# A small VectorE instruction with a destination in three rows instead of one run

## The chip, the core and the metric

The kernel runs on one core of a Trainium2 chip. A core has five engines that work side by side, each through its own list of instructions in a fixed order: TensorE (PE in the profile; its weight loads are PEld), VectorE (DVE), ScalarE (ACT), GpSimd (POOL) and SyncE (SP, which here issues most of the DMAs). They wait for one another through semaphores. The metric is the time of one execution on the device, in microseconds. Before the change it is 1541.81 us, the median of three runs (1540.87 to 1546.98).

## The reference

Two steps, one behind the other: attention that keeps the 32 largest scores of each row, and a mixture of eight experts on its output.

```python
def _attn_ref(q, k, v):                      # q, k, v: (8, 8, 576, 64)
    scores = scale * np.matmul(q, k.transpose(0, 1, 3, 2))
    kth = np.partition(scores, -32, axis=-1)[..., -32:-31]
    mask = scores >= kth
    scores = np.where(mask, scores, -1e9)
    ...                                      # softmax over the kept scores
    return np.matmul(attn, v)

def _moe_ref(x, w_gate, w1, w2):             # x: (4608, 512), 8 experts
    logits = x @ w_gate
    order = np.argsort(-logits.flatten())    # greedy: best pairs first, at most 576 tokens an expert
    ...
    out[mask] = np.maximum(x[mask] @ w1[e], 0.0) @ w2[e]   # for each expert
```

## The kernel before

**Stages.** The attention takes the first 1076 us or so, then come the routing and the experts. The change touches the attention alone.

**Tiles.** The 64 heads are taken in 32 pairs. The two heads of a pair have 2 x 576 rows of scores, that is nine tiles of 128 rows and 576 columns; tile 4 holds the last 64 rows of both heads. Each tile goes through the same steps (function `tile_ops`). The names in brackets are those that rows of the trace show, with their lines:

- TensorE writes the scores to PSUM (`s`, L449), in f16 pairs of high and low parts. Four such score areas are in use at a time.
- VectorE takes the eight largest of each of six chunks of 96 columns (`cd`, L453 and L454), and out of these 48 candidates the eight largest three times, blanking what it has found in between (MAX8 at L457, L459, L461, MATCH_REPLACE8 at L458, L460). So it has the 24 largest in `st`.
- ScalarE marks with a sign which scores lie above the 24th (`w`, L466) and adds the signs up in a column of `acc`: with them it is known how many scores reach the threshold.
- VectorE makes the **fill** (`fw`, L476): it compares a small table `tab` of constants with that column. The result are eight numbers, each 0 or a tiny negative one.
- TensorE pushes the marked scores far down (`s<-w,off`, L471), and adds the fill, multiplied by the same large constant (`s<-fw,off`, L472), to eight spare columns beside the scores.
- VectorE takes the eight largest of the 584 columns that are now there (MAX8, L473). They end with the 32nd largest score.
- ScalarE makes a mask of what lies under it (`r`, L479). TensorE turns scores and masks round and adds them up (`pt`, L515 to L521), ScalarE takes the exponential (`F`, L525), and GpSimd splits it into high and low f16 parts (`ehm`, L528, and `elm`, L531). TensorE multiplies these with the values (`pv`, L622).

**A loop over three tiles.** The largest score of a row, known after L457, goes into the queries that the turned products use. For every three tiles of a pair GpSimd copies the maxima into the queries (`nq`, L500), and a DMA on SyncE's queue transposes them (`Qt<-nq`, L501). Products of later tiles read them (`s<-kz,Qt`, L449). So a pair has three such transposes, 96 in all.

**What sets the order.** A planner (class `Loom`) sorts the operations of each engine by a table of numbers (`TAU`), one list for each engine, and the program is issued in that order. Within an engine the order is fixed; only semaphores decide when an instruction starts. The planner adds spare matmuls where TensorE would stand idle for long (function `stay`).

**Buffers.** The fill's tile has four buffers, the table is made once, at the kernel's start, by an iota on GpSimd.

Of the kernel before, what the change touches and what calls it, by code (L numbers as in the profile page):

```python
# [9 lines left out]
F32 = mybir.dt.float32  # L10
F32R = mybir.dt.float32r
F16 = mybir.dt.float16
BF16 = mybir.dt.bfloat16
# [3 lines left out]
ALU = mybir.AluOpType  # L17
# [193 lines left out]
def attention(tc, q,k,v,w_gate,x_out,L,acc,cuts, pairs,ahead=()):  # L211
# [3 lines left out]
    with ExitStack() as ctx:  # L215
        ctx.enter_context(tc.manual_schedule())
        cp=ctx.enter_context(tc.tile_pool(name="cp",bufs=1))
        io=ctx.enter_context(tc.tile_pool(name="io",bufs=2))
        wk=ctx.enter_context(tc.tile_pool(name="wk",bufs=2))
# [3 lines left out]
        V,G,A,T=nc.vector,nc.gpsimd,nc.scalar,nc.tensor  # L223
        SS=[ps_s.tile([128,1536],F32,name=f"s{j}") for j in range(LANES//2)]
        def part(slot,kind,x,e):

            j,a=slot%(LANES//2),slot//(LANES//2)
            tc.add_to_no_dep_group(f"{j}{a}{kind}{e}",x.ins)
            for g in {"o":(f"{j}{1-a}o",f"{j}{1-a}m",f"{j}{1-a}t",f"{j}{a}t"),"t":(f"{j}{1-a}o",f"{j}{a}o"),"m":(f"{j}{1-a}o",)}[kind]:
                for o in "VAP":  # L230
                    if o!=e: tc.declare_no_dep(x.ins,group=g+o,reason="another bank")
            return x
        identf=cp.tile([128,128],F32,name="identf"); make_identity(nc,identf)
        off=cp.tile([128,128],BF16,name="off"); V.tensor_scalar_mul(off,identf,-(2.0**79))
        out_=cp.tile([128,128],BF16,name="out_"); V.tensor_scalar_mul(out_,identf,-(2.0**48))
        keep=cp.tile([128,128],BF16,name="keep"); V.tensor_scalar_mul(keep,identf,2.0**127)

        tab=cp.tile([128,8],F32,name="tab")
        G.iota(tab,[[2,8]],base=2*24-576,channel_multiplier=0,allow_small_or_imprecise_dtypes=True)
        wg=cp.tile([128,4,8],F32,name="wg")  # L240
        wgr=cp.tile([128,2,2,8],F32,name="wgr")
        wv=w_gate.rearrange("(g r a d) e -> a r d g e",g=2,r=2,a=2,d=64)
# [5 lines left out]
        for i in range(2):  # L248
            t=cp.tile([128,2,9,128],F16,name=f"nq{i}"); NQ.append(t); V.memset(t[:,1,:,64:128],0.0)
            t=cp.tile([128,2,9,128],F16,name=f"nk{i}"); NK.append(t); V.memset(t[:,1,:,65:128],0.0); V.memset(t[:,1,:,64:65],-QS)  # L250
# [178 lines left out]
        def tile_ops(P,i):  # L429
# [3 lines left out]
            col=slice(n*9+i,n*9+i+1)  # L433
            D={}
            def at_(): return D["at"]["slot"]
            def side(): return at_()//(LANES//2)
            def span(a,b):

                s_ps=SS[at_()%(LANES//2)]; o=960*side()
                return s_ps[:,o+a:o+b]  # L440
# [4 lines left out]
            def products(Q,K,n_,o,k0,kind,first,last):  # L445
                for h in ([0] if i<4 else ([1] if i>4 else [0,1])):
                    if i==4: rows=slice(h*64,h*64+64); qc=slice(512+h*64,576+h*64)
                    else: rows=slice(0,128); qc=slice(i*128,i*128+128)
                    part(at_(),kind,T.matmul(o[rows],P[Q][:n_,qc],P[K][:n_,k0(h):k0(h)+o.shape[1]],start=first,stop=last,skip_group_check=True),"P")  # L449
# [17 lines left out]
            def move(half):  # L467
                u=side(); o=64*u if half else 512*(1-u); n_=512 if half else 64
                if not half:
                    for Q,K,k0 in (("Q1","K2",512),("Q2","KZ",0)): products(Q,K,128,span(o,o+64),lambda h: k0+64*h,"t",Q=="Q1",False)  # L470
                part(at_(),"o" if half else "t",T.matmul(span(o,o+n_),off,P["w"][i][:,o:o+n_],start=False,stop=bool(half),skip_group_check=True),"P")  # L471
                if not half: part(at_(),"t",T.matmul(span(-8,0) if u else span(576,584),off,D["fw"],start=False,stop=True,skip_group_check=True),"P")  # L472
            def next8(): part(at_(),"m",V.max(P["st"][:,i,24:32],span(-8,576) if side() else span(0,584)),"V")  # L473
            def fill():
                D["fw"]=wk.tile([128,8],BF16,tag="fw",name="fw",bufs=4)
                V.tensor_scalar(D["fw"],tab,acc[:,col],-2.0**-39,op0=ALU.is_lt,op1=ALU.mult)  # L476
            def relu():
                r=wk.tile([128,576],BF16,tag="r",name="r",bufs=WPB); P["r"][i]=r
                part(at_(),"m",A.activation(r,span(0,576),AF.Relu,bias=P["st"][:,i,31:32],scale=-1.0),"A")  # L479
# [8 lines left out]
            p=go("nt",minus,[p],e="A",d=.092,late=.1)  # L488
            p=tw=go("sg",sign,[p],take="w",e="A",d=0.717); mid.append(p)
            f_=go("fl",fill,[p],e="V",d=.11)  # L490
            p=go("o0",lambda: move(1),[p],e="P",d=.218)
            p=go("o1",lambda: move(0),[p,f_,P["kz"]],e="P",d=.125 if i==4 else .093,m=i==4); mid.append(p)
            p=go("y8",next8,[p],e="V",d=0.69); mid.append(p)
            p=go("rl",relu,[p],take="r",free=[ts],e="A",d=.63); P["tr"][i]=[p,tw]; mid.append(p)
# [882 lines left out]
def attention_then_moe(tc, q, k, v, w_gate, w1, w2, out):  # L1377
    with ExitStack() as ctx:
        dp = ctx.enter_context(tc.tile_pool(name="dp", bufs=1, space=DRAM))
        lp = ctx.enter_context(tc.tile_pool(name="lp", bufs=1))  # L1380
        x = dp.tile([4608, 512], F32, name="x")
        Lx = lp.tile([128, 37, 8], F32, name="L"); L = Lx[:, 0:36, :]
        pairs = [(b, hp) for b in range(8) for hp in range(4)]
        flags = lp.tile([1, 40], I32, name="flags")
        K = moe_consts(tc, lp)
        acc = lp.tile([128, len(pairs) * 9], F32, name="acc")
        cuts = lp.tile([128, 2, len(pairs) * 9], F32, name="cuts")
        tail = dict(idx=lp.tile([128, 5], I32, name="idx7"), ob=lp.tile([128, 512], F32, name="ob7"))
        attention(tc, q, k, v, w_gate, x, L, acc, cuts, pairs, rows_ahead(tc, lp, K, Lx))
        moe(tc, K, L, x, w1, w2, out, tail, (acc, cuts, flags))  # L1390
        def last(to=out): tc.nc.gpsimd.indirect_dma_start(out=to, out_offset=bass.IndirectOffsetOnAxis(ap=tail["idx"][:, 3:4], axis=0), in_=tail["ob"], in_offset=None)  # L1391
        redo(tc, q, k, v, w_gate, x, L, flags, tail["any"], lambda: moe(tc, K, L, x, w1, w2, out, tail), last, tail["rows"])
# [27 lines left out]
```

## Time and profile before

| | |
|---|---|
| median of the runs | 1541.81 us (1540.87 to 1546.98, 3 runs) |
| the profiled execution's own time | 1534.06 us |
| its span, first to last instruction | 1532.3 us |
| granted TensorE clock, mean over the span | 0.949 |
| VectorE busy | 1209.8 us, 79% |
| TensorE busy | 1296.1 us, 85% |
| fills (L476), all 288 | 180.6 us, 627 ns each |
| attention, 20 to 1076 us: VectorE busy | 886.33 of 1056 us |

All durations come from one profiled execution. A row of the page or of an answer names line, engine, operation and tiles as `out<-in`; times are us unless marked ns. Times in the timeline count from the span's start. In square brackets behind a row stands how long the engine was idle before it, and who ended that. Busy time of an instruction runs from its start to its end. VectorE's instructions overlap a little: the next one may start before the last one has ended.

### The profile page before, as it was taken

To read this page: it belongs to the slowest core of one execution; us is meant where nothing else is said; L and a number is where in the kernel's file an instruction comes from. 1 tells how busy PE (TensorE), PEld (TensorE's weight loads), DVE (VectorE), ACT (ScalarE), POOL (GpSimd) and SP (SyncE) were. 2 spreads that over 40 slices of the span, in tenths; PEclk is the share of its full clock that TensorE was granted. 3 is DMA by queue.
4 is the path that set the end of the run, shared out by engine and by line. 5 is a ranking of instruction groups with operands and counts; after the bars stand their busy time and mean duration, and the time that the engine had idled before them with its cause. 6 is when DMAs were issued, how large, how long until landed. Compare 5 with 4: busy or idle time off the path is not lost. (4 is left out here: it accounts for less than half of the span.)

```text
span 1532.3 us, 45618 instructions
## 1 busy us (share of the span) xinstructions
PE 1296.1 (85%) x17276; PEld 961.0 (63%) x17277; DVE 1209.8 (79%) x5557; ACT 941.5 (61%) x2177; POOL 821.5 (54%) x1090
## 2 busy tenths in 40 slices
PE   7778878788778778888878787878788999999998
PEld 5666666666666666666656666666674666566654
DVE  7888788788878888888878888889498989895411
ACT  3776777677777767777767777777234444235411
POOL 3766767667676767676766767676112222222011
PEclk9998999889999999999999999999799999999999
DMA  5343344324334442433433343341147656658000
GB/s 113 74 77 69 67 95 89 80 64 109 67 66 95 89 79 64 113 66 64 106 82 75 67 110 66 72 103 30 40 142 199 183 186 196 189 186 224 29 32 34
DMA packets 313130, 148.97 MB, mean 97 GB/s; under 512 B 278532, under 2 KB 294916, under 8 KB 311876
## 3 DMA queue, kind: packets, MB, share of 16 engines
q1 hardware_dynamic: 306530, 126.53, 35.0%
q0 software_dynamic: 5968, 19.14, 4.0%
q8 instruction: 137, 2.24, 0.6%
q14 instruction: 93, 0.76, 0.2%
q10 hardware_dynamic: 402, 0.29, 0.1%
HBM read 71.60 MB, written 18.87 MB: 59 GB/s over the span
## 5 line engine op out<-in xcount | busy, mean ns | idle before, releaser
L453 DVE MAX8 cd<-s 128x8 f32<-128x96 f32 x1440 | 316.5, 249 | 11.6 <-PE s L449 10.2
L449 PEld LDWEIGHTS <-Qt 128*128 128x128 f16 (+1 forms) x1920 | 149.6, 105 | 274.7 <-DMA Qt<-nq 178.3
L449 PE MATMUL s<-Kt,Qt 128*128 128x64 f16 (+3 forms) x1600 | 288.5, 280 | 19.1 <-ACT w L466 8.5
L479 ACT ACTIVATE r<-s,st 128x576 bf16<-128x576 f32 x288 | 210.9, 740 | 134.3 <-DVE st L473 122.8
L531 POOL TENSOR_TENSOR elm<-F,ehm 128x512 f16<-128x512 f32 x253 | 287.3, 1156 | 0.3
L473 DVE MAX8 st<-s 128x8 f32<-128x584 f32 x288 | 215.5, 757 | 82.4 <-PE s L472 80.1
L466 ACT ACTIVATE w<-s,st 128x576 uint16<-128x576 f32 x288 | 214.1, 744 | 65.0 <-PE s L472 54.9
L528 POOL TENSOR_SCALAR ehm<-F 128x512 f16<-128x512 f32 x253 | 153.9, 616 | 168.6 <-ACT F L525 167.5
L1269 PE MATMUL ph<-xT,w1h 128*128 128x288 f16 (+1 forms) x1024 | 190.0, 286 | 3.8 <-DMA xT<-xs 3.8
L449 PE MATMUL s<-kz,Qt 128*128 128x64 f16 (+1 forms) x320 | 58.4, 206 | 158.7 <-DMA Qt<-nq 158.5
L521 PE MATMUL pt<-Qt,Kt 65*128 65x128 f16 (+1 forms) x1280 | 180.9, 220 | 0.1
L476 DVE TENSOR_SCALAR fw<-tab,acc 128x8 bf16<-128x8 f32 x288 | 180.6, 627 | 0.2
L520 PE MATMUL pt<-Qt,Kt 128*128 128x128 f16 (+1 forms) x1280 | 180.5, 219 | 0.0
L1329 POOL DMA_INDIRECT out_dram<-ob,idx x39 | 41.9, 1075 | 238.0 <-ACT ob L1324 221.3
L525 ACT ACTIVATE F<-pt 128x512 f32<-128x512 f32 x256 | 149.4, 595 | 14.3 <-PE pt L521 11.3
L471 PE MATMUL s<-w,off 128*128 128x512 f16 (+1 forms) x576 | 156.0, 302 | 0.3 <-ACT w L466 0.2
L1269 PE MATMUL ph<-xT,w1l 128*128 128x288 f16 (+1 forms) x512 | 146.0, 286 | 0.0
L520 PEld LDWEIGHTS <-Kt 128*128 128x128 f16 x1280 | 121.5, 101 | 15.5 <-issue 11.7
L515 PEld LDWEIGHTS <-r 128*128 128x128 bf16 x1280 | 88.9, 102 | 59.4 <-issue 37.1
L454 DVE MAX8 cd<-s 128x8 f32<-128x96 f32 x288 | 72.4, 251 | 68.0 <-PE s L449 59.4
L622 PE MATMUL pv<-vh,ehm 128*128 128x65 f16 x1012 | 124.1, 199 | 1.3 <-DVE xb L640 0.4
L622 PE MATMUL pv<-vh,elm 128*128 128x65 f16 x1012 | 124.4, 198 | 0.0
(314 smaller groups left out, 3725.2 us busy)
## 6 DMA issues: line engine op xcount, KB each, us to landing
wr<-in_moe_w_dram SPq DMA_DIRECT2D x32, 1024.0 KB
kn<-in_k_dram SPq DMA_DIRECT2D x32, 256.0 KB
vt<-in_v_dram SPq DMA_DIRECT2D x64, 128.0 KB
x<-xb SPq DMA_DIRECT2D x8, 1024.0 KB
qn<-in_q_dram SPq DMA_DIRECT2D x31, 256.0 KB
Qt<-nq SPq DMA_TRANSPOSE x129
kn<-in_k_dram SPq DMA_DIRECT2D x32, 32.0 KB
vt<-in_v_dram SPq DMA_DIRECT2D x64, 16.0 KB
```

The lines of the kernel that those rows point to most:

```text
L449: part(at_(),kind,T.matmul(o[rows],P[Q][:n_,qc],P[K][:n_,k0(h):k0(h)+o.shape[1]],start=first,stop=last,skip_group_check=True),"P")
L453: if c<5: part(at_(),"o",V.max(o,main(512-CW-CW*c,512-CW*c) if u else main(CW*c,CW*c+CW)),"V")
L466: part(at_(),"m",A.activation(D["w"],span(0,576),AF.Sign,bias=P["st"][:,i,32:33],scale=(1+2.0**-21),accum_out=acc[:,col]),"A")
L471: part(at_(),"o" if half else "t",T.matmul(span(o,o+n_),off,P["w"][i][:,o:o+n_],start=False,stop=bool(half),skip_group_check=True),"P")
L473: def next8(): part(at_(),"m",V.max(P["st"][:,i,24:32],span(-8,576) if side() else span(0,584)),"V")
L476: V.tensor_scalar(D["fw"],tab,acc[:,col],-2.0**-39,op0=ALU.is_lt,op1=ALU.mult)
L479: part(at_(),"m",A.activation(r,span(0,576),AF.Relu,bias=P["st"][:,i,31:32],scale=-1.0),"A")
L520: T.matmul(o,K2[:,kb:kb+128],Q1[:,qc],start=False,stop=False,skip_group_check=True)
L521: T.matmul(o,K3[0:65,kb:kb+128],Q2[0:65,qc],start=False,stop=(c==3 and h==sub[-1][0]),skip_group_check=True)
L531: G.tensor_tensor(el,D["E"],D["eh"],op=ALU.subtract); P["e"][i]=(D["eh"],el)
L622: for m_ in (range(N-3) if part==0 else range(N-3,N)): T.matmul(out,seq[m_][0],seq[m_][1],start=(m_==0),stop=(m_==N-1))
L1269: P.matmul(B["ph"][:,lo-c0:hi-c0],a[:,c,fs],xT[:,b+c,lo:hi],start=(i==0),stop=(i==11),skip_group_check=True)
```

## The change

The table has twelve columns in place of eight, the tile for the fill is [128, 3, 8] in place of [128, 8], and the fill is written into the first four columns of each of its three rows: twelve numbers, in three runs of four with gaps of four. The matmul reads the first four columns of the first two rows, which hold the same eight numbers as before; the third row is read by nobody. The numbers that reach PSUM are the same. No instruction is added or taken away, and none changes its place: the lists of TensorE, ScalarE and SyncE are the same row for row, that of VectorE has 128x3x4 in place of 128x8 at each of the 288 fills, and GpSimd's differs in the iota's size.

```diff
-        tab=cp.tile([128,8],F32,name="tab")
-        G.iota(tab,[[2,8]],base=2*24-576,channel_multiplier=0,allow_small_or_imprecise_dtypes=True)
+        tab=cp.tile([128,12],F32,name="tab")
+        G.iota(tab,[[2,12]],base=2*24-576,channel_multiplier=0,allow_small_or_imprecise_dtypes=True)
...
-                if not half: part(at_(),"t",T.matmul(span(-8,0) if u else span(576,584),off,D["fw"],start=False,stop=True,skip_group_check=True),"P")
+                if not half: part(at_(),"t",T.matmul(span(-8,0) if u else span(576,584),off,D["fw"][:,0:2,0:4],start=False,stop=True,skip_group_check=True),"P")
...
             def fill():
-                D["fw"]=wk.tile([128,8],BF16,tag="fw",name="fw",bufs=4)
-                V.tensor_scalar(D["fw"],tab,acc[:,col],-2.0**-39,op0=ALU.is_lt,op1=ALU.mult)
+                D["fw"]=wk.tile([128,3,8],BF16,tag="fw",name="fw",bufs=4)
+                V.tensor_scalar(D["fw"][:,:,0:4],tab,acc[:,col],-2.0**-39,op0=ALU.is_lt,op1=ALU.mult)
```

## Rows read from the trace of the kernel before

**Rows 1.** The page's first part: engine, busy us, share of the span, instructions.

```profile
PE 1296.1 (85%) x17276; PEld 961.0 (63%) x17277; DVE 1209.8 (79%) x5557; ACT 941.5 (61%) x2177; POOL 821.5 (54%) x1090
```

**Rows 2.** Windows: from:to, length, busy of PE PEld DVE ACT POOL, clock, DMA.

```profile
20.00:1076.00 1056.00, 852.38 (x13605) 665.59 (x13603) 886.33 (x4533) 774.21 (x1884) 721.94 (x971) 0.94 0.37 80
...
505.00:508.00 3.00, 2.00 (x38) 1.55 (x37) 2.75 (x6) 0.74 (x1) 2.98 (x6) 1.00 0.77 147
...
700.00:800.00 100.00, 81.94 (x1270) 63.89 (x1271) 82.24 (x424) 72.38 (x176) 69.06 (x93) 0.90 0.39 83
...
769.00:772.00 3.00, 1.89 (x24) 1.49 (x25) 1.34 (x5) 0.57 (x1) 2.40 (x4) 0.62 0.92 175
...
800.00:900.00 100.00, 79.60 (x1313) 61.90 (x1309) 84.99 (x432) 74.15 (x181) 69.36 (x94) 0.97 0.39 86
```

**Rows 3.** Lines L476 and L458: ns min/median/max, first and last start.

```profile
L476 DVE TENSOR_SCALAR fw<-tab,acc x288: 208/527/1970, 21.8 to 1074.1; 128x8 bf16<-128x8 f32 x144
...
L458 DVE MATCH_REPLACE8 cd<-st,cd x288: 183/193/201, 18.4 to 1067.5; 128x48 f32<-128x48 f32 x144
```

**Rows 4.** Waits: engine and line, who ended them, total us, times, longest.

```profile
PE s L449 <- DMA Qt<-nq: 160.2, 87, 3.9
...
DVE st L473 <- PE s L472: 80.1, 39, 3.6
...
PE s L472 <- DVE fw L476: 23.8, 49, 1.2
```

**Rows 5.** VectorE's instructions grouped by line: busy us, mean ns, idle before.

```profile
L476 DVE TENSOR_SCALAR fw<-tab,acc 128x8 bf16<-128x8 f32 x288 | 180.6, 627 | 0.2
```

**Rows 6.** Timeline of VectorE and GpSimd at two fills: start, us, instruction.

```profile
506.18 1.83 DVE L476 TENSOR_SCALAR fw<-tab,acc 128x8 bf16<-128x8 f32 x1
...
526.89 0.22 DVE L476 TENSOR_SCALAR fw<-tab,acc 128x8 bf16<-128x8 f32 x1
...
505.47 1.35 POOL L375 TENSOR_TENSOR vl<-vs,vh 128x640 f16<-128x640 f32 x1
506.79 1.19 POOL L528 TENSOR_SCALAR ehm<-F 128x512 f16<-128x512 f32 x2
...
526.50 0.14 POOL L385 MEMSET nq<- 128x9 f16 x1
```

**Rows 7.** Windows of L476 alone, one pair each: DVE busy, clock, DMA.

```profile
500.00:533.00 33.00, 5.90 (x9) 1.00 0.36 77
...
766.00:799.00 33.00, 5.58 (x9) 0.90 0.36 77
```

**Rows 8.** Timeline of the first pair, rows of DVE, PE, POOL and ACT.

```profile
501.54 0.70 DVE L476 TENSOR_SCALAR fw<-tab,acc 128x8 bf16<-128x8 f32 x1
...
505.25 0.77 DVE L473 MAX8 st<-s 128x8 f32<-128x584 f32 x1 [2.24 <-PE s L472]
...
508.06 0.17 PE L472 MATMUL s<-fw,off 128*128 128x8 bf16 x1 [1.06 <-DVE fw L476]
...
509.88 0.62 POOL L528 TENSOR_SCALAR ehm<-F 128x512 f16<-128x512 f32 x1 [1.89 <-ACT F L525]
...
518.01 0.74 ACT L479 ACTIVATE r<-s,st 128x576 bf16<-128x576 f32 x1 [0.56 <-DVE st L473]
...
526.16 1.41 ACT L479 ACTIVATE r<-s,st 128x576 bf16<-128x576 f32 x2 [0.40 <-DVE st L473]
```

**Rows 9.** Timeline of the second pair, rows of POOL, DVE and ACT.

```profile
777.06 0.20 POOL L500 TENSOR_SCALAR nq<-st 128x3 f16<-128x3 f32 x1 [0.23 <-DVE st L457]
...
780.76 0.27 DVE L454 MAX8 cd<-s 128x8 f32<-128x96 f32 x1 [0.26 <-PE s L472]
...
791.60 1.41 ACT L479 ACTIVATE r<-s,st 128x576 bf16<-128x576 f32 x2 [0.46 <-DVE st L473]
```

**Rows 10.** Timeline of TensorE: the first matmul behind two long waits.

```profile
504.83 0.22 PE L449 MATMUL s<-kz,Qt 128*64 128x64 f16 x2 [2.59 <-DMA Qt<-nq]
...
770.11 0.27 PE L449 MATMUL s<-kz,Qt 128*64 128x64 f16 x2 [2.99 <-DMA Qt<-nq]
```

## The prediction

> **What bounds the kernel now.** I read the page's busy shares first, then the windows, then the one line that the diff touches, then the waits, and last the timeline of two stretches of one pair each.
>
> The shares [rows 1] show no engine at its limit over the whole span. The windows show where the line under change runs: the attention stage, 20 to 1076 us, where VectorE is the fullest engine with 886 of 1056 us, ahead of TensorE (852), ScalarE (774) and GpSimd (722) [rows 2]. The fill (L476) runs 288 times, nine per pair of heads, all between 21.8 and 1074.1 us [rows 3], so what comes after attention keeps its time. Nobody is at 100%, because the engines work in fixed order and hand each tile round: the longest waits are TensorE's for the transposed queries (160.2 us) and VectorE's for TensorE (80.1 us) [rows 4]. Time taken off VectorE therefore counts only where somebody stands waiting for VectorE.
>
> The fill itself is odd. It makes 8 numbers per partition, yet takes 627 ns in the mean and 180.6 us in all [rows 5]. Its shortest is 208 ns, its median 527, its longest 1970, while a MATCH_REPLACE8 over 48 numbers, also between SBUF tiles, stays between 183 and 201 ns in all 288 cases [rows 3]. The timeline tells what stretches it [rows 6]. The fill that starts at 506.18 us ends at 508.01; GpSimd works in that time without a pause, one instruction from 505.47 to 506.82 and two from 506.79 to 507.98, and the fill ends as GpSimd's last one ends. The fill at 526.89, which starts after GpSimd's memset has ended at 526.64, takes 0.22. So the fill waits for GpSimd to stand still, and VectorE, which works in order, stands with it. The MATCH_REPLACE8 run beside the same GpSimd work and do not wait, so it is something in the form of the fill.
>
> **The change part by part.**
>
> *The iota* over 12 columns in place of 8 is one GpSimd instruction before the stage; I cost it at nothing, since it stands long before the first fill.
>
> *The fill's form.* One run of 8 in and out becomes one run of 12 in and three rows of 4 out that don't touch. No row of before shows such an instruction. Lower bound: 208 ns, the fill without a wait [rows 3]; upper bound: today's 627 ns, if the wait stays. The four further columns are too few to matter: MATCH_REPLACE8 moves 48 in 193 ns. I take the lower end, because the nearest row of an instruction that never waits is at 193. What goes is then 180.6 − 288 × 0.208 = 180.6 − 59.9 = 120.7 us of VectorE's time, 0.42 per fill.
>
> [...]
>
> *The matmul that reads the fill* takes rows 0 and 1, the same eight values in two pieces of 4; still one instruction of 8 columns. I cost it at nothing.
>
> *Order.* No instruction changes its place on any engine, and no wait is added.
>
> *How much of the 120.7 us is on the path.* Bounds from the waits [rows 4]: at least the 23.8 us in which TensorE stood for a fill by name; at most all 120.7. Between them I walk two pairs by hand and count, once for each stall, the idle time of another engine that VectorE's lateness caused.
>
> First pair, 500 to 533 us: nine fills take 5.90 us, 5.90 − 9 × 0.208 = 4.03 above the least [rows 7]. The fill at 501.54 (0.70) buys nothing: VectorE finishes what it has and then idles 2.24 us until 505.25 for TensorE [rows 8]. The long one at 506.18 holds TensorE idle for 1.06 us at 508.06 [rows 8]; that frees the products behind the exponentials for which GpSimd waits at 509.88 (1.89 us, for ScalarE) [rows 8], and after which GpSimd copies the maxima out for the next transpose. VectorE itself would be 1.6 us earlier, but TensorE had only 1.06 to give, so 1.06 counts. In the second third ScalarE waits 0.56 us at 518.01 for VectorE, in the last third 0.40 at 526.16 [rows 8], both behind fills. Sum 1.06 + 0.56 + 0.40 = 2.02, half of 4.03.
>
> Second pair, 766 to 799 us: 5.58 − 1.87 = 3.71 us above the least [rows 7]. GpSimd waits 0.23 us for VectorE at 777.06 before the copy of the maxima; VectorE idles 0.26 at 780.76 for TensorE anyway, so what is saved in that third is lost again; ScalarE waits 0.46 for VectorE at 791.60 [rows 9]. Sum 0.69, a fifth of 3.71.
>
> Together 2.71 of 7.74 us, 35%, or 1.355 us per pair. Over 32 pairs that is 43.4 us, between the bounds 23.8 and 120.7. I take it as it is: second-order gains (a wait that shrinks because its cause was itself late) and second-order losses (a stall that TensorE or GpSimd fills instead) are not seen in such a walk and may go either way.
>
> What is late next: TensorE's wait for the transposed queries, which hangs on GpSimd's copy and a DMA that don't get faster. GpSimd's own work doesn't shorten: its instructions run back to back while the fill waits.
>
> *The sum.* The profiled execution took 1534.06 us, its span 1532.3 and 1.8 around it; 1534.1 − 43.4 = 1490.7. The runs shown have a median of 1541.81, 7.8 us above it, so the forecast for the median is 1541.8 − 43.4 = 1498 us, 2.8% less.
>
> **The rivals.**
>
> *Little arrives.* Fixed order and the DMA decide, and only TensorE's direct waits for fills, 23.8 us [rows 4], or less come back: 1518 to 1534. For it: the second pair, and the 160.2 us for the queries. Against it: the first pair, and VectorE being the fullest engine.
>
> *Nearly all arrives.* VectorE is the bound wherever it doesn't idle, so 70 to 120.7 us come back: 1421 to 1472. For it: 84% of the stage busy [rows 2]. Against it: four engines lie between 68 and 84%, so TensorE, at 81%, takes over soon.
>
> *The wait stays.* The new form still waits for GpSimd, and the change does nothing: 1541 to 1543. For it: no row of before shows the form. Against it: the other VectorE instructions between SBUF tiles that pass GpSimd unhindered [rows 3].
>
> *Slower, by TensorE's clock.* The stalls for the transposed queries hang on GpSimd and a DMA. If VectorE and TensorE come to them earlier, each stall grows, and the clock falls behind it. [...] Against it: after the 2.59 us at 504.83 [rows 10] it is 1.00 from 505 to 508 [rows 2], so the stall alone doesn't decide. The price, from two stretches of 100 us: 1270 matmuls at 0.90, 1313 at 0.97 [rows 2], 3.4% for 0.07, on 1056 us some 36 us, or 5.1 us per hundredth. To eat 43.4 us and cost 0.5% more (7.7), the stage's clock must fall by 51 / 5.1 = ten hundredths, from 0.94 to below 0.84; from there it decides, and the time is 1550 or more.
>
> **How the numbers follow.** Forecast (20 to 70 us gained): 0.60. Nearly all: 0.10. Little (8 to 20 us): 0.12. The wait stays, or all of it is lost in other waits: 0.11. Slower by the clock: 0.07. Within 0.5% (7.7 us) is what a measurement of this kernel can't tell from no change; so faster 0.82, same 0.11, slower 0.07. The range leaves out the slower case (0.07), most of no change (0.08) and the far half of "nearly all" (0.04): gains of 4 to 90 us, 1452 to 1538. The likeliest case's own range is 1472 to 1522.
>
> **What would show it.** Right: fills of about 0.21 us with a longest near their median, some 60 us in all, and none ending with GpSimd's instruction; TensorE's wait for fills near zero; VectorE idle for longer, with its waits for TensorE grown; the matmul, ScalarE and GpSimd groups of the attention stage unchanged in busy time; the stage some 43 us shorter, and the same time after it. Wrong in its first step: fills still up to 1.9 us. Wrong in its second: fills short, but the stage shortened by less than 20 or more than 70 us; then the waits for the transposed queries should have grown by what is missing, or shrunk. Wrong by the clock: a granted clock of the stage well under 0.94.

## The result and the profile after

The changed kernel takes 1500.53 us, the median of four runs (1494.74 to 1508.69), against 1541.99 us for the kernel before (four runs): 0.9729 of the time, with a 95% interval of 0.9672 to 0.9786. That is 41.5 us less. The forecast was 1498 us, 43.4 less.

The page's first part, as in [rows 1]:

```profile
PE 1280.0 (86%) x17276; PEld 954.3 (64%) x17277; DVE 1102.4 (74%) x5557; ACT 934.4 (63%) x2177; POOL 822.2 (55%) x1090
```

Only VectorE stands out, with 1102.4 us in place of 1209.8. The window of the attention, in the columns of [rows 2], up to where it now ends:

```profile
20.00:1036.00 1016.00, 834.89 (x13612) 657.96 (x13610) 778.87 (x4534) 766.96 (x1884) 722.46 (x972) 0.94 0.39 83
```

VectorE's busy time in the attention falls from 886.33 [rows 2] to 778.87 us, by 107.5; the stage falls from 1056 to 1016, by 40. The other 67.5 us are now VectorE's idle time (1056 − 886.3 = 169.7 before, 1016 − 778.9 = 237.1 after). ScalarE's and GpSimd's busy times stay within 1%, and TensorE's granted clock reads 0.94 in both. TensorE's busy time falls by 17.5 us (2%); this was not taken apart.

The line that was changed, and the MATCH_REPLACE8 beside it, as in [rows 3]:

```profile
L476 DVE TENSOR_SCALAR fw<-tab,acc x288: 202/209/225, 22.0 to 1034.6; 128x12 bf16<-128x12 f32 x144
...
L458 DVE MATCH_REPLACE8 cd<-st,cd x288: 184/193/196, 18.5 to 1029.7; 128x48 f32<-128x48 f32 x144
```

And the fills grouped by line, as in [rows 5]:

```profile
L476 DVE TENSOR_SCALAR fw<-tab,acc 128x12 bf16<-128x12 f32 x288 | 60.6, 211 | 0.4 <-ACT w L466 0.2
```

The longest fill is 225 ns where it was 1970; it reads the column of `acc` as before. The stretch from the first to the last fill was 1074.1 − 21.8 = 1052.3 us and is 1034.6 − 22.0 = 1012.6. The fill that answers to the long one of [rows 6], the same one of the 288, from the timelines of VectorE and GpSimd:

```profile
485.02 0.21 DVE L476 TENSOR_SCALAR fw<-tab,acc 128x12 bf16<-128x12 f32 x1
485.15 0.20 DVE L461 MAX8 st<-cd 128x8 f32<-128x48 f32 x1
...
484.05 1.35 POOL L375 TENSOR_TENSOR vl<-vs,vh 128x640 f16<-128x640 f32 x1
485.37 1.20 POOL L528 TENSOR_SCALAR ehm<-F 128x512 f16<-128x512 f32 x2
```

GpSimd works through the whole fill, at the same three instructions as before, and the fill takes 0.21 us; VectorE's next instruction starts 0.13 us behind its start.

The reading that a long fill waits for GpSimd holds for more than this one. Counted over the trace of the kernel before, 199 of the 288 fills take longer than 0.25 us, and each of them ends 25 to 32 ns behind the end of a GpSimd instruction. After the change none takes that long.

Where the time went is told by the waits, in the form of [rows 4]:

```profile
PE s L449 <- DMA Qt<-nq: 171.2, 95, 3.9
...
ACT r L479 <- DVE st L473: 120.2, 65, 4.0
...
DVE st L473 <- PE s L472: 100.8, 38, 4.2
```

TensorE waits for no fill any more (23.8 us before). VectorE's wait for TensorE grew from 80.1 to 100.8 us, and TensorE's for the transposed queries from 160.2 to 171.2. ScalarE's wait for VectorE, which the hand-walk had counted on to shrink, stands at 120.2; before it was:

```profile
ACT r L479 <- DVE st L473: 122.8, 120, 3.5
```

### The profile page after: what moved, and what is told of

It is laid out like the page before. It is cut to its first block, busy times and chain, and to the rows that moved or that the text cites. A ratio compares the mean times of both kernels' runs of the same rounds, so it can differ in the third digit from the quotient of the medians.

```text
span 1494.7 us, 45618 instructions
## 1 busy us (share of the span) xinstructions
PE 1280.0 (86%) x17276; PEld 954.3 (64%) x17277; DVE 1102.4 (74%) x5557; ACT 934.4 (63%) x2177; POOL 822.2 (55%) x1090
## 5 line engine op out<-in xcount | busy, mean ns | idle before, releaser
L449 PEld LDWEIGHTS <-Qt 128*128 128x128 f16 (+1 forms) x1920 | 149.7, 105 | 264.6 <-DMA Qt<-nq 189.2
L473 DVE MAX8 st<-s 128x8 f32<-128x584 f32 x288 | 216.8, 762 | 117.3 <-PE s L472 100.8
L449 PE MATMUL s<-Kt,Qt 128*128 128x64 f16 (+3 forms) x1600 | 289.5, 282 | 11.2 <-ACT w L466 8.1
L479 ACT ACTIVATE r<-s,st 128x576 bf16<-128x576 f32 x288 | 210.5, 739 | 130.9 <-DVE st L473 120.2
L449 PE MATMUL s<-kz,Qt 128*128 128x64 f16 (+1 forms) x320 | 58.2, 206 | 169.3 <-DMA Qt<-nq 169.3
L525 ACT ACTIVATE F<-pt 128x512 f32<-128x512 f32 x256 | 148.8, 594 | 43.4 <-PE pt L521 39.9
L622 PE MATMUL pv<-vl,ehm 128*128 128x65 f16 x1012 | 124.4, 198 | 0.0
L520 PEld LDWEIGHTS <-Kt 128*128 128x128 f16 x1280 | 120.7, 101 | 4.4 <-issue 0.7
L521 PEld LDWEIGHTS <-Kt 65*128 65x128 f16 x1280 | 120.5, 100 | 4.1 <-issue 0.3
```

The lines of the kernel that those rows point to most:

```text
L520: T.matmul(o,K2[:,kb:kb+128],Q1[:,qc],start=False,stop=False,skip_group_check=True)
L521: T.matmul(o,K3[0:65,kb:kb+128],Q2[0:65,qc],start=False,stop=(c==3 and h==sub[-1][0]),skip_group_check=True)
L622: for m_ in (range(N-3) if part==0 else range(N-3,N)): T.matmul(out,seq[m_][0],seq[m_][1],start=(m_==0),stop=(m_==N-1))
```

## The experiments

Each was timed beside the kernel before on the same chip, and is compared by its ratio to it: the kernel before takes 1547.8, 1550.1 and 1551.9 us on the three chips of the experiments.

**What in the form lets the fill pass: three other forms.** The first writes the twelve columns in one run. Its cut is set against the kernel before, all later ones against the changed kernel:

```diff
-                D["fw"]=wk.tile([128,8],BF16,tag="fw",name="fw",bufs=4)
+                D["fw"]=wk.tile([128,12],BF16,tag="fw",name="fw",bufs=4)     # tab has 12 columns; the matmul reads 0:8
```

> Twelve columns, but written as one run of 12 (source 12, destination 12). Theory A, the wait goes because the counts of source and destination (12 and 3) no longer fit together: the waits stay, fills with a median near 500 ns, a longest above 1500, some 180 us in all, time 1535 to 1550. Rival B, the larger count does it: all fills near 0.21 us, 60 us in all, time near 1500. Rival C, the gaps in the destination do it: waits stay, as in A. [...]

The second keeps eight columns and writes two rows of four with gaps:

```diff
-        tab=cp.tile([128,12],F32,name="tab")
+        tab=cp.tile([128,8],F32,name="tab")          # the iota likewise
...
-                D["fw"]=wk.tile([128,3,8],BF16,tag="fw",name="fw",bufs=4)
+                D["fw"]=wk.tile([128,2,8],BF16,tag="fw",name="fw",bufs=4)
```

> Eight columns, written as two rows of four with gaps (source one run of 8, destination 2 rows). Theory A, counts that fit together (8 and 2, both even): the waits stay, median near 500 ns, 180 us in all, time 1535 to 1550. Rival C, gaps in the destination are enough: fills near 0.21 us, 60 us in all, time near 1500. Rival B, the larger count: waits stay.

The third writes exactly what the changed kernel writes, but reads the table from three rows with gaps:

```diff
-        tab=cp.tile([128,12],F32,name="tab")
+        tab=cp.tile([128,3,8],F32,name="tab")        # the iota fills it so that [:,:,0:4] has the same twelve numbers
...
-                V.tensor_scalar(D["fw"][:,:,0:4],tab,acc[:,col],-2.0**-39,op0=ALU.is_lt,op1=ALU.mult)
+                V.tensor_scalar(D["fw"][:,:,0:4],tab[:,:,0:4],acc[:,col],-2.0**-39,op0=ALU.is_lt,op1=ALU.mult)
```

> The destination as in the changed kernel, three rows of four with gaps, but the table too lies in three rows of four with gaps, so that source and destination have 3 rows each. Theory A, counts that fit together (3 and 3, odd and equal): the waits are back, median near 500 ns, 180 us in all, time 1535 to 1550. Rival C, gaps in the destination are enough: fills near 0.21 us, time near 1500. Rival D, an odd outermost count is enough: fills near 0.21 us, time near 1500.

Line L476 of the first, ns min/median/max:

```profile
L476 DVE TENSOR_SCALAR fw<-tab,acc x288: 207/544/2148, 22.3 to 1090.3; 128x12 bf16<-128x12 f32 x144
```

Of the second:

```profile
L476 DVE TENSOR_SCALAR fw<-tab,acc x288: 207/516/2037, 21.7 to 1084.3; 128x8 bf16<-128x8 f32 x144
```

Of the third:

```profile
L476 DVE TENSOR_SCALAR fw<-tab,acc x288: 205/540/1971, 21.8 to 1078.5; 128x12 bf16<-128x12 f32 x144
```

All three have the waits back, as long as in [rows 3] (183.9, 181.8 and 180.6 us of fills in all), and all three take the time of before: ratios 1.0024 (0.9998 to 1.005), 0.9981 (0.9949 to 1.0013) and 0.9975 (0.9944 to 1.0006). The first, at 1551.6 us, lies 1.6 above the times expected, on a chip where the kernel before takes 1547.8. So theory A holds in each, and the rivals fall: it is not the count of twelve (first), not gaps in the destination (second), and not an odd number of rows in it (third, whose destination is the changed kernel's to the byte). With 8 and 8, 12 and 12, 8 and 2, or 3 and 3 as outermost counts of source and destination the fill waits (up to 1.97, 2.15, 2.04 and 1.97 us); with 12 and 3 it does not (at most 0.225 us). These five pairs are all that was tried. The traces show who waits and for how long; why the counts matter they do not show.

**An even load in place of the waits.** Three more fills ahead of each, into tiles that nobody reads:

```diff
             def fill():
+                for z in range(3): V.tensor_scalar(wk.tile([128,3,8],BF16,tag="fx",name="fx",bufs=6)[:,:,0:4],tab,acc[:,col],-2.0**-39,op0=ALU.is_lt,op1=ALU.mult)
```

(In the kernel it stands within line L475, so that all later lines keep their numbers.)

> The changed kernel with three more fills of the same form ahead of each fill, into tiles that nobody reads. The next instruction starts 0.13 us after such a fill, so this puts 3 x 0.13 = 0.40 us on VectorE per tile, 115 us in all, as much as the waits took (180.6 - 59.9 = 121 us), but spread evenly and without GpSimd. Theory E, a third of VectorE's time lies on the path, however it is spread: 35 to 45 us longer than the changed kernel, 1530 to 1545. Rival F, the cost was in the few long waits and VectorE's idle time hides an even load: 0 to 20 us longer, 1495 to 1520. Rival G, an even load is worse, since waits behind idle time cost nothing before: 50 us longer or more, 1550 and up.

Measured: ratio 0.9916 (0.9878 to 0.9953), that is 0.9916 / 0.9729 = 1.019 of the changed kernel, or 29 us more; with both intervals about 18 to 39. From its timeline:

```profile
502.01 0.48 DVE L475 TENSOR_SCALAR fx<-tab,acc 128x12 bf16<-128x12 f32 x3
502.40 0.22 DVE L476 TENSOR_SCALAR fw<-tab,acc 128x12 bf16<-128x12 f32 x1
```

Three of them push the fill by 0.39 us, 288 × 0.39 = 112 us in all. Of these 29 arrive, 0.26. The waits cost 41.5 for 120.0 us, 0.35. None of the three theories had this size: E, "however it is spread", asked for at least 35, F for at most 20, G for 50. The intervals don't tell the even load from the waits. The window of the attention even puts them close:

```profile
20.00:1072.10 1052.10, 862.73 (x13623) 672.25 (x13621) 883.37 (x5398) 784.49 (x1884) 722.54 (x972) 0.93 0.38 80
```

The load adds 104.5 us to VectorE's busy time of 778.87 and 36 us to the stage of 1016; the waits had added 107.5 and 40.

**No fills.** One tile of zeros is read in the fills' place:

```diff
             def fill():
-                D["fw"]=wk.tile([128,3,8],BF16,tag="fw",name="fw",bufs=4)
-                V.tensor_scalar(D["fw"][:,:,0:4],tab,acc[:,col],-2.0**-39,op0=ALU.is_lt,op1=ALU.mult)
+                D["fw"]=fw0
```

> The changed kernel without the 288 fills: one tile of zeros, made at the start, is read in their place (the fills' values are left out; they are zero wherever no scores tie at the 24th place). That takes 288 x 0.13 = 37 us more off VectorE. Theory F, after the change VectorE is hardly on the path: 0 to 10 us less than the changed kernel, ratio to before 0.965 to 0.975. Rival E, a third or a quarter of VectorE's time still lies on the path: 9 to 13 us less, ratio 0.963 to 0.967. Since these lie close, the waits decide: under F, ScalarE's wait for VectorE (120 us in the changed kernel) shrinks by less than 10 us, under E by more.

Measured: ratio 0.9731 (0.9691 to 0.9772), the changed kernel's. Leaving out the fills brings nothing that can be seen, with some 11 us of uncertainty either way from both intervals. Of its waits

```profile
PE s L449 <- DMA Qt<-nq: 171.1, 94, 4.5
...
ACT r L479 <- DVE st L473: 136.9, 83, 4.3
```

the one for VectorE is longer, not shorter, than 120.2. By the expectation's own measure this sides with F. It doesn't settle the matter, as the window shows:

```profile
20.00:1052.00 1032.00, 849.48 (x13623) 668.60 (x13619) 758.21 (x4248) 762.94 (x1885) 722.61 (x973) 0.92 0.39 81
```

VectorE's busy time fell by 20.7 us, not 37, so E would have given back some 5 to 7; and TensorE's clock is 0.92 where the changed kernel had 0.94, which by the prediction's price of 5.1 us per hundredth (an estimate from two stretches of 100 us [rows 2]) is 10 us, more than that. (The fills are not zero nearly everywhere, as the expectation supposed; what this kernel leaves out is their values. The instructions that read them are all there.)

**Where the rest of the 120.7 us went.** TensorE's longest wait was for the transposed queries, 171.2 us in the changed kernel. The products of the last columns (L449, kz) read the tile that the DMA has just overwritten, although they don't need the maxima in it: the row of the maxima meets zeros in kz. So the DMA is given a tile of its own, and only the turned products read it:

```diff
-                def q2(): nc.sync.dma_start_transpose(P["Q2t"][:,i0:i0+3,:],...)
+                def q2(): nc.sync.dma_start_transpose(later()[:,i0:i0+3,:],...)     # later(): io.tile([128,9,128],F16,tag="qm",bufs=2)
...
-                Q1,Q2,K2,K3=P["Q1"],P["Q2"],P["K2"],P["K3"]
+                Q1,Q2,K2,K3=P["Q1"],P["Q2m"],P["K2"],P["K3"]                        # likewise for tile 4's products
```

It was put into the changed kernel and into the kernel before.

> The changed kernel, with the queries that hold the maxima transposed into a tile of their own, so that the products with the last columns (L449, kz) read the old tile and need not wait for that DMA (171 us of TensorE's waits in the changed kernel); only the turned products (L521) read the new one. Theory H, the rest of the gain (121 us off VectorE, 41 us arrived) was held by this wait: TensorE's wait for the transposed queries nearly goes, and the time falls by 40 us or more below the changed kernel, ratio to before under 0.945. Rival I, the wait moves to L521 or to GpSimd and ScalarE: less than 20 us, ratio 0.96 to 0.973.

> The same separate tile in the kernel before, where the fills wait for GpSimd. Theory H: with the transposes' wait out of the way, VectorE is the bound, so the waiting fills cost more than the 41 us: this kernel is 60 to 100 us slower than the one with the separate tile and short fills, and gains less against before (0 to 30 us). Rival I: the two kernels differ by 41 us or less, as without the separate tile.

Measured: 0.8648 (0.8614 to 0.8682), 1339.6 us, with the short fills; 0.917 (0.9133 to 0.9207), 1420.8 us, with the waiting ones. They differ by 81 us. The same change that is worth 41.5 us is worth 81 where the transposes hold TensorE less: rival I (41 us or less) falls, and theory H's difference of 60 to 100 us is met. H missed in two other numbers. It let the waiting kernel gain 0 to 30 us against before, and it gains 129. And the separate tile brought the changed kernel 168 us (0.1081 of 1550.1), twice the 80 us or so that H was to find there; so the wait held up more than the rest of this change's gain. The first of the two is also faster than either kernel of this case, by 13.5% against before and 11% against the changed one. Its window of the attention:

```profile
20.00:869.50 849.50, 791.90 (x13618) 634.79 (x13615) 770.80 (x4534) 762.35 (x1884) 715.82 (x972) 0.98 0.48 99
```

Its waits:

```profile
DVE cd L453 <- PE s L449: 53.5, 39, 4.3
...
PE s L449 <- DMA Qt<-nq: 47.6, 32, 2.9
...
ACT r L479 <- DVE st L473: 16.6, 42, 1.0
```

TensorE is busy 791.9 of 849.5 us, 93% where it was 81% [rows 2], and its wait for the queries is 47.6. The stage got shorter than the changed kernel's by 166.5 us, more than the wait that went (171.2 − 47.6 = 123.6); ScalarE's wait for VectorE fell too, from 120.2 to 16.6, and the clock rose from 0.94 to 0.98. How much each of these gave was not taken apart.

In the one with waiting fills the line of the fills reads:

```profile
L476 DVE TENSOR_SCALAR fw<-tab,acc x288: 203/730/3517, 21.9 to 955.8; 128x8 bf16<-128x8 f32 x144
```

Their group:

```profile
L476 DVE TENSOR_SCALAR fw<-tab,acc 128x8 bf16<-128x8 f32 x288 | 208.1, 723 | 1.6
```

And who waits for them:

```profile
PE s L472 <- DVE fw L476: 84.1, 104, 3.4
```

Its window of the attention:

```profile
20.00:957.70 937.70, 833.12 (x13614) 655.49 (x13613) 907.76 (x4533) 769.15 (x1884) 719.57 (x971) 0.96 0.43 90
```

GpSimd does the same work in less time, so it is busy for 77% of the stage where it was 68% [rows 2], and a fill takes up to 3.5 us. TensorE stands 84.1 us for fills where it stood 23.8 [rows 4]. VectorE, its waits included, is busy 97% of the stage, which is close to the bound that H named.

**The even load once more**, in the fast version:

```diff
             def fill():                                             # with the separate tile and short fills
+                for z in range(3): V.tensor_scalar(...)             # as above
```

> The kernel with the separate tile and short fills, with the three more fills ahead of each fill: 115 us more on VectorE, spread evenly. Theory J, with the transposes' wait gone VectorE's time itself decides: 70 to 115 us slower than without them (1340 there), ratio to before 0.91 to 0.94, as much as the waiting fills (81 us) or more. Rival K, what costs is the uneven wait that ties VectorE to GpSimd, and an even load is cheaper, as it was without the separate tile (29 against 41 us): 30 to 60 us slower, ratio 0.885 to 0.905.

Measured: 0.8824 (0.8792 to 0.8855), that is 1.020 of the version without the load, 27 us, with both intervals 20 to 34. The time lies under both ranges and nearest to K; J's size falls. Per microsecond 112 us spread evenly cost 27, or 0.24, and the waits of 208.1 − 288 × 0.203 = 149.6 us cost 81, or 0.54. But this doesn't show that an even load is cheaper, as K has it. Its window:

```profile
20.00:907.50 887.50, 823.27 (x13608) 643.32 (x13606) 870.24 (x5398) 773.39 (x1884) 717.98 (x972) 1.00 0.47 95
```

Without either, VectorE is idle for 849.5 − 770.8 = 78.7 us of the stage. The even load makes it 99.4 us busier, and its idle time falls to 17.3; the waits make it 137.0 us busier, and its idle time falls to 29.9. So the idle time takes up 61.4 and 48.8 us, and the rest lengthens the stage, by 38.0 and 88.2. Of the 50.2 us between the two, 37.5 are the waits' larger time and 12.7 are idle time that the even load used better. So the costs differ mostly because the waits are more of VectorE's time, and less because they are uneven. TensorE's clock differs as well, 1.00 under the load, 0.98 without and 0.96 with the waits; by 5.1 us per hundredth (the prediction's estimate) that is some 10 us in favour of the load, and 10 against the waits. (The windows are of single executions, and the one without either is the fastest of its five.)

TensorE's wait for the fills under the even load:

```profile
PE s L472 <- DVE fw L476: 14.6, 47, 0.6
```

It is 14.6 us, none longer than 0.6, where the waiting fills made it 84.1, up to 3.4. Whether the length of the single wait costs something by itself, at the same time of VectorE in all, was not tried.

## Why the prediction was right

*The form.* That the wait would go, and leave about 0.21 us, was right: 120.7 us forecast, 180.6 − 60.6 = 120.0 measured. VectorE's busy time fell by less, 107.5; the difference was not taken apart. That the form would pass was a choice between two bounds, and no row of before showed it. The reason given, the nearest row that never waits, would not have told the changed form from the three that were tried; the counts of source and destination do. That a fill "waits for GpSimd to stand still" was too strong. Of the 199 long fills 90 end where the next GpSimd instruction follows within 0.1 us, like this one, which ends at 514.46 behind the first of three in a row:

```profile
513.54 0.92 DVE L476 TENSOR_SCALAR fw<-tab,acc 128x8 bf16<-128x8 f32 x1
...
513.27 3.38 POOL L531 TENSOR_TENSOR elm<-F,ehm 128x512 f16<-128x512 f32 x3
```

The fill at 506.18 did otherwise: it came before two of GpSimd's three instructions and still ended behind the last [rows 6].

*How much arrives.* The hand-walk said 43.4; the medians say 41.5, the stage 40. The walk's share, 35% of the waits, came out at 41.5 / 120.0 = 35%. Over all pairs the last copy of the maxima (L500) comes every 33.10 us before and every 31.87 after, 1.23 less where the walk had 1.355 (31 steps, from 41.37 to 1067.46 us and from 41.57 to 1029.66). The steps can be checked against the same pair in the profile after, which begins at 483.45 us. The rows are TensorE's restarts behind the transposed queries, and GpSimd's last copy of the maxima. Timeline before:

```profile
514.44 0.20 PE L449 MATMUL s<-kz,Qt 128*128 128x64 f16 x1 [0.58 <-DMA Qt<-nq]
...
523.46 0.20 PE L449 MATMUL s<-kz,Qt 128*128 128x64 f16 x1 [1.71 <-DMA Qt<-nq]
...
533.30 0.21 POOL L500 TENSOR_SCALAR nq<-st 128x3 f16<-128x3 f32 x1
```

Timeline after:

```profile
483.45 0.27 PE L449 MATMUL s<-kz,Qt 128*64 128x64 f16 x2 [2.42 <-DMA Qt<-nq]
...
492.45 0.20 PE L449 MATMUL s<-kz,Qt 128*128 128x64 f16 x1 [0.49 <-DMA Qt<-nq]
...
500.74 0.20 PE L449 MATMUL s<-kz,Qt 128*128 128x64 f16 x1 [1.56 <-DMA Qt<-nq]
...
510.15 0.22 POOL L500 TENSOR_SCALAR nq<-st 128x3 f16<-128x3 f32 x1
```

From the first restart to the second it is 514.44 − 504.83 = 9.61 us before [rows 10] and 9.00 after, 0.61 less, where the walk had 1.06. To the third 9.02 and 8.29, 0.73 less (0.56). To the last copy 9.84 and 9.41, 0.43 less (0.40). Sum 1.77, forecast 2.02. But the first third's gain is not where the walk put it. From the first restart to the matmul that had stood 1.06 us for the fill it is 508.06 − 504.83 = 3.23 us before [rows 8, rows 10] and 486.70 − 483.45 = 3.25 after: TensorE doesn't stand there any more, but it works at a lower clock for a part of that time, 0.73 in the mean of the six microseconds. The window:

```profile
483.00:489.00 6.00, 5.55 (x82) 4.49 (x83) 4.25 (x22) 3.31 (x10) 4.43 (x8) 0.73 0.52 100
```

And from its timeline:

```profile
484.71 1.04 PE L449 MATMUL s<-Kt,Qt 128*128 128x512 f16 x2
...
486.70 0.17 PE L472 MATMUL s<-fw,off 128*128 128x8 bf16 x1
...
490.14 0.59 PE L449 MATMUL s<-Kt,Qt 128*128 128x512 f16 x2
```

Two matmuls of 512 columns take 1.04 us at a clock of 0.50 (484.71 to 485.75 us) where they take 0.59 later, at 1.00 (490.14 to 490.73). The pair before had 1.00 from 505 to 508 us; the second pair of the forecast had a stretch at a lower clock, too, 0.62 from 769 to 772 [rows 2]. The 0.61 us that did come in this third came behind it, where the walk had counted nothing.

*What was luck.* Two pairs of 32 gave shares of 50% and 19%; that their mean hit owes something to chance. From pair to pair the copies' spacing changed by anything from 2.6 us more to 4.0 less. In the pair that can be followed the largest term, 1.06, was taken up by the clock, and other gains stood in for it. And 1.42 of the 2.71 us walked were waits of ScalarE for VectorE, which in the sum didn't shrink (122.8 to 120.2 us). How far each third moves up the walk got about right; that these waits themselves would be gone was wrong. In the sum they came back, and they are fewer and longer (65 up to 4.0 us, where they were 120 up to 3.5).

*The rivals.* "The wait stays" was real: three forms that look much alike do nothing. The changed fill does not share it: none takes longer than 225 ns. "Little arrives" and "nearly all arrives" differ by what else stands in the way: with the transposes' wait the change brings 41.5 us, with most of it gone 81. The slower case did not come: the clocks of each hundred microseconds from 100 to 1000 us lie between 0.90 and 0.97 before and after, and the stage's mean reads 0.94 in both. Of the two long stalls in [rows 10], the one of 2.99 us has a clock of 0.62 at its end (769 to 772 us), the one of 2.59 us a clock of 1.00 behind it (505 to 508) [rows 2]. TensorE's wait for the queries grew by 11 us, as said.

## What to carry to other kernels

Here an instruction whose shortest and median durations lie far apart (208 and 527 ns), with ends that fall on another engine's ends (25 to 32 ns behind them), was waiting, though the profile calls it busy; look for a form that needn't wait before moving it. In the five forms tried, what decides is the pair of outermost counts of source and destination (a longest fill of 0.225 us with 12 and 3, of 1.97 or more with the four others), so this small fill could be freed by four more columns that nobody reads. What the freed time was worth hung here on the next wait of the loop, a transpose that wrote into a tile still needed (41.5 us with it, 81 with most of it gone), and it paid to take that away as well: alone the two were worth 41.5 and 129 us (1550.1 − 1420.8), together 210.5 (1550.1 − 1339.6), more than their sum. VectorE's idle time took up 61.4 of the 99.4 us that the even load added to its stage in the version with the separate tile: compare busy and idle time of the stage before calling one kind of load cheaper than another.

## What the runs showed of the hardware that was not expected

- A waiting fill sometimes goes on past the end of a GpSimd instruction behind which another follows: the one of [rows 6] outlasts the ends of two, and 34 of the 199 long ones outlast at least one. But 90 of them end where another follows within 0.1 us. The longest fills are 1.97 us before and 3.52 in the version with the separate tile. Which of the two happens was not tried.
- GpSimd's busy time doesn't show the waits: in the attention it is 721.94 us with them [rows 2] and 722.46 without.
- In the version with the separate tile, VectorE's idle time of 78.7 us took up 61.4 us of an even load and 48.8 us of the waits; only what went beyond that lengthened the stage.
